# Spreading the normalisation steps of a first projection stage, and reordering the loads of output weights where a recurrent chain begins

## The chip, the cores and the metric

The kernel runs on one core of a Trainium2 chip. The metric is the device time of one launch in microseconds (us). Of several launches the median is compared.

## The reference

Four layers alternate, A B A B, each added to a residual stream of 2048 rows of 640 values. The change touches layer A: a recurrent transformer with memory. Rows come in 64 segments of 32; every segment is preceded by 8 memory rows, which are the first 8 output rows of the segment before.

```python
for s in range(n_seg):                       # 64 segments, one after the other
    xs = x[:, s * seg_len:(s + 1) * seg_len, :]      # x is the layer norm of the stream
    h = jnp.concatenate([mem, xs], axis=1)           # 8 + 32 rows
    q, k, v = (einsum('btd,dhe->bhte', h, W) for W in (Wq, Wk, Wv))   # 32 heads of 192
    scores = jnp.where(mask, einsum('bhqe,bhke->bhqk', q, k) * scale, -1e9)
    o = einsum('bhqk,bhke->bhqe', softmax(scores), v)
    o = einsum('bhte,hed->btd', o, Wo)
    mem = o[:, :M, :]
    outs.append(o[:, M:, :])
```

Layer B is linear attention with softmax features (32 heads of 20) and stays as it is.

## The kernel before

Each layer A has two parts. `A_pre` is a batched stage: it projects the last 8 rows of every segment (the tail rows 24 to 31) to Q, K and V, for all 64 segments at once, so that the chain has only 32 rows left to project per segment: the 8 memory rows and rows 0 to 23. `A_chain` is the chain over the 64 segments.

**The batched stage.** The 64 segments are two halves, h = 0 and 1, of 32 segments; each half's 256 tail rows are gathered from DRAM, normalised (in layer 0 only, where `x_raw` is given), transposed on TensorE (`transpose_rows`, tile `pt`) and stand as `xT[h]` in SBUF. The heads are four rounds r of 8 heads. So there are 8 steps (h, ri): in layer 0 both halves of r = 3, then of r = 2, 1 and 0. This document numbers them 0 to 7. A step projects K, then Q (12 PSUM banks of 10 matmuls of 256 columns, L803), stores both with one DMA from ACT's queue (`kqb`, L809, 1536 KB, from staging buffer `sts[step % 2]`), then V (8 banks of 5 matmuls of 384 columns, L820), stored by POOL's DMAs (`vb`, L824, from the staging buffers `vts`). All matmul banks come from one pool of 8. `evict` copies a bank to its staging buffer, on DVE and ACT in turn (L87 and L89), and then runs one entry of a list `tasks`, if there is one.

In layer 0 that list holds side steps: first the normalisation of the second half's tail rows (`tails`), then that of all 2048 rows in 16 blocks of 128 (`all_rows`), whose result goes to DRAM for the chain. One block is four entries: a starts the load of x on POOL's queue (L755), b takes the moments (DVE L221 and L223, then two casts on POOL, L225 and L227), c takes Ln and Exp on ACT (L234, L235), d applies them on DVE (L241 to L244) and stores (POOL, L756). The entry a of the next block stands ahead of b of this one. Both halves are transposed when their first step begins.

**Weights.** SP's queue loads the matrices in the order of their use, in pieces of 384 KB (L625 for places used once, L619 for the nine slots that r = 3, r = 0 and later the chain share). It runs far ahead of TensorE. `wo_rows` is a copy of two quarters of the output weights Wo (r = 0 and 3) to a DRAM tensor of another layout; it is two DMAs of 1920 KB from ACT's queue (L649), at step 4. The chain then loads Wo in pieces of 320 KB: r = 0 and 3 from `wo_rows` into `wo_end` (L636), r = 1 and 2 from the input into `wo_mid` (L638). During the stage `wo_end` holds `vts` and `xT` and `wo_mid` holds `sts`, so a piece (r, k) can be loaded only when its place comes free. The set `early` names those that are loaded in the last step (`early_wo`); the others are loaded when the chain begins (`late_wo`), ahead of the slots that its first segment needs next. At the chain's first segment, between Q and K of its first round, `fill(FILL[li])` issues short weight loads on TensorE.

**The order of things.** This part of the kernel is scheduled by hand: each engine and queue runs in the order of the program. A DMA from SP or from ACT carries one of eight completion semaphores (`DMAHW0` to `DMAHW7`, shared by both), and the program makes its issue wait until the transfer that had that semaphore before has landed. What stands behind a waiting issue on the same engine waits with it, and on ACT those are copies out of PSUM.

Of the kernel before, what the change touches and what calls it, by code (L numbers as in the profile page):

```python
# [8 lines left out]
P = 128  # L9
BF16 = mybir.dt.bfloat16  # L10
F32 = mybir.dt.float32
# [8 lines left out]

FILL = {0: 122, 2: 78}
SEG_FILL = 1
# [93 lines left out]
class Kernel:  # L116
# [98 lines left out]

    def ln_moments(self, lp, xt):
        nc, Dm = self.nc, self.Dm
        half = Dm // 2
        stats = lp.tile([P, 2, 6], F32, name="ln_stats")
        for j in range(2):  # L220
            nc.vector.bn_stats(out=stats[:, j, :], in_=xt[:, j * half:(j + 1) * half])  # L221
        mv = lp.tile([P, 2], F32, name="ln_mv")
        nc.vector.bn_aggr(out=mv[:], in_=stats[:])  # L223
        mv16 = lp.tile([P, 2], BF16, name="ln_mv16")
        nc.gpsimd.tensor_copy(out=mv16[:], in_=mv[:])  # L225
        mvr = lp.tile([P, 2], F32, name="ln_mvr")
        nc.gpsimd.tensor_copy(out=mvr[:], in_=mv16[:])  # L227
        return mvr
# [352 lines left out]
    def layer_A(self, xn_dram, at_dram, li, x_raw=None):  # L581
# [46 lines left out]

        early = {(0, 5), (2, 4), (2, 5), (1, 0), (1, 1), (1, 2), (1, 3)}

# [14 lines left out]
        def lay_out_wo():  # L645
            if li == 0:
                self.wo_rows = dram.tile([2, P, 7680], BF16, name="wo_rows")
                for i, r in enumerate((0, 3)):
                    nc.scalar.dma_start(out=self.wo_rows[i].rearrange("p (c m) -> p c m", m=640),  # L649
                                        in_=wov[:, 12 * r:12 * r + 12, :])  # L650

        def early_wo():
            for r in (0, 2, 1):
                load_wo(r, part=[k for k in range(6) if (r, k) in early])

        def late_wo(r):
            load_wo(r, part=[k for k in range(6) if (r, k) not in early])

# [9 lines left out]
    def A_pre(self, xn_dram, li, load_matrix, piece, wo_mid, wo_end, lay_out_wo, early_wo, x_raw):  # L668
# [12 lines left out]
        with ExitStack() as es:  # L681
# [4 lines left out]
            else:  # L686
                es.enter_context(tc.manual_schedule(engines={nc.sync.engine}))
            xT = [wo_end[:, 3584 + 1280 * i:3584 + 1280 * i + 1280] for i in range(2)]
            xB = None
# [22 lines left out]
            def norm_tasks(load, done, tag="ln_xn"):  # L712

                v = {}

                def a():
                    v["x"] = lp.tile([P, self.Dm], BF16, name="ln_x")
                    load(v["x"])

                def b():  # L720
                    v["m"] = self.ln_moments(lp, v["x"])

                def c():
# [18 lines left out]
            def evict(out, in_):  # L742
                ev.copy(out=out, in_=in_)
                if tasks:
                    tasks.pop(0)()

            normed = {}

            def tails(h):
                return in_turn([norm_tasks(lambda x, k=k: gather(x, x_raw, h, k),  # L750
                                           lambda xn, k=k: normed.__setitem__((h, k), xn), "ln_xt") for k in range(NT)])

            def all_rows():
                rows = [slice(P * b, P * b + P) for b in range(self.NB)]
                return in_turn([norm_tasks(lambda x, q=q: nc.gpsimd.dma_start(out=x[:], in_=x_raw[q, :]),  # L755
                                           lambda xn, q=q: nc.gpsimd.dma_start(out=xn_dram[q, :], in_=xn[:]))  # L756
                                for q in rows])
# [15 lines left out]
            for h, ri, r in steps:  # L773
                if h not in seen:
                    seen.add(h)
                    xBT = columns(h)
                    for k in range(NT):
                        if x_raw is not None:
                            xb = normed[h, k]
                        else:  # L780
                            xb = xB[h][k % 2]
                            gather(xb, xn_dram, h, k)
                        transpose_rows(xb, h, k)
                xBT = columns(h)
                if (h, ri) == ((NH - 1, 0) if x_raw is None else (0, 2)):
                    lay_out_wo()
# [27 lines left out]
                for k in range(NT):  # L814
                    vt = vts[nv % 2]
                    nv += 1
                    for g in range(4):
                        ps = ps_.tile([P, 512], F32, name="ps_pre", tag="bank")
                        for b in range(KC):
                            nc.tensor.matmul(ps[:, 0:384], lhsT=xBT[:, b, P * k:P * k + P],  # L820
                                             rhs=w[b][:, 384 * g:384 * g + 384], start=(b == 0), stop=(b == KC - 1))
# [8 lines left out]
    def A_chain(self, xn_dram, at_dram, li, load_slot, piece, load_wo, late_wo, wo_mid, wo_end, low):  # L830
# [3 lines left out]
        with tc.tile_pool(name=f"A{li}_ch", reuse_waits="tile", bufs=1) as sp, \  # L834
# [358 lines left out]
```

## Time and profile before

| | us |
|---|---|
| median of 4 runs (3764.53 to 3778.69) | 3772.76 |
| the profiled execution: its time | 3764.53 |
| the profiled execution: its span | 3762.8 |
| layer 0: batched stage, from the first projection to the chain's first matmul | 11.26 to 197.46 |
| layer 0: the chain's first segment | 197.46 to 234.07 |
| its second segment | 234.07 to 255.01 |
| layer 2: end of the batched stage, and the chain's first segment | 2061.18, 2061.18 to 2097.56 |

Times within the profile are us from the span's start. Step 5, 6 and 7 of the batched stage start at 138.56, 158.16 and 177.76. The span's time and the launch's time differ by 1.7 us.

### The profile page before, as it was taken

How to read it: one execution, taken by the hardware profiler on the slowest of the kernel's cores; microseconds unless marked ns; L12 is line 12 of the kernel's file. 1: busy time of each engine (PE TensorE's matmuls, PEld its weight loads, DVE VectorE, ACT ScalarE, POOL GpSimd, SP SyncE). 2: the span in 40 equal slices, each digit the busy share in tenths (PEclk: the TensorE clock that was granted, in tenths of full speed). 3: DMA queues.
4: the chain of work that ended last, by engine and by line, in shares of the span. 5: the costliest groups of instructions: out<-in, count | busy, mean ns of one | idle time of the engine just before them, and what ended most of it. 6: DMA issues, size and time to landing. Idle time of an engine off the chain costs nothing.

```text
span 3762.8 us, 169123 instructions
## 1 busy us (share of the span) xinstructions
PE 3550.7 (94%) x71064; PEld 2322.1 (62%) x71408; DVE 2364.3 (63%) x6290; ACT 2075.1 (55%) x5285; POOL 1660.1 (44%) x4363
## 2 busy tenths in 40 slices
PE   7989999999999999989899899999999999999898
PEld 5756666666666666555377566666666666665453
DVE  5456666666666667546633566666666666664565
ACT  2246566666666656546433556666666666655453
POOL 3345555555555545430333445555545555543400
PEclk9999999999999999989899999999999999999899
DMA  9788788887888878830477888888887888879200
GB/s 348 222 275 290 273 285 289 278 297 271 291 285 286 292 261 296 296 105 1 143 252 203 291 274 293 278 295 276 290 283 271 293 278 288 290 264 309 64 1 29
DMA packets 531381, 931.72 MB, mean 248 GB/s; under 512 B 141034, under 2 KB 298362, under 8 KB 530618
## 3 DMA queue, kind: packets, MB, share of 16 engines
q1 hardware_dynamic: 392794, 802.36, 60.8%
q0 software_dynamic: 68160, 88.78, 8.1%
q10 hardware_dynamic: 69664, 29.76, 3.0%
q8 instruction: 558, 9.14, 1.0%
q14 instruction: 205, 1.68, 0.1%
HBM read 852.43 MB, written 72.09 MB: 246 GB/s over the span
## 4 chain that ended last, share of the span: by engine, by line
PE 55%; DMA 16%; DVE 7%; issue 7%; ACT 6%; PEld 5%; POOL 3%; SPq 1%; POOLq 0%; ACTq 0%; DVEq 0%
PE ps_qk L901 18%; DMA arena<-wo_rows 8%; PE ps_w L977 7%; PE ps_v L901 7%; PE ps_o L951 4%; PE ps_s L943 4%; PEld L803 3%; DMA arena<-in_A_Wv_dram 3%; PE ps_s L1009 2%; PE ps_idle L984 2%; PE ps_s L938 2%; DVE hT L857 2%; PE ps_qk L388 2%; DMA Vp<-vb 1%; PE ps_pre L803 1%
## 5 line engine op out<-in xcount | busy, mean ns | idle before, releaser
L901 PE MATMUL ps_qk<-arena,hT 128*32 128x384 bf16 x20480 | 1001.8, 328 | 25.0 <-DMA arena<-in_A_Wk_dram 11.4
L901 PEld LDWEIGHTS <-hT 128*32 128x32 bf16 x30720 | 738.9, 96 | 443.4 <-DVE hT L1119 27.0
L911 ACT ACTIVATE raw<-ps_qk 128x384 bf16<-128x384 f32 x1024 | 503.1, 491 | 399.0 <-PE ps_s L1009 248.8
L977 PE MATMUL ps_w<-arena,OT 128*32 128x160 bf16 x24576 | 546.9, 235 | 27.9 <-issue 15.8
L884 POOL DMA_DIRECT2D Vp<-vb x512 | 258.8, 506 | 671.7 <-PE ps_o L951 460.1
L901 PE MATMUL ps_v<-arena,hT 128*32 128x384 bf16 x10240 | 535.1, 329 | 0.0
L977 PEld LDWEIGHTS <-OT 128*32 128x32 bf16 x24576 | 437.2, 97 | 123.9 <-issue 46.3
L916 DVE STREAM_TRANSPOSE KT<-raw 128x384 bf16<-128x384 bf16 x512 | 296.1, 578 | 205.3 <-ACT raw L911 201.3
L919 DVE STREAM_TRANSPOSE QT<-raw 128x256 bf16<-128x256 bf16 x512 | 227.9, 445 | 240.2 <-ACT raw L911 199.5
L872 POOL DMA_DIRECT2D kqb<-kqb x512 | 286.1, 559 | 162.9 <-POOL KT L880 148.5
L932 DVE CAST Vp<-ps_v 64x384 bf16<-64x384 f32 x512 | 286.1, 559 | 88.9 <-ACT Vp L930 75.6
L970 POOL DMA_DIRECT2D otb<-otb x512 | 282.9, 552 | 121.5 <-DVE otb L966 101.9
L930 ACT ACTIVATE Vp<-ps_v 64x384 bf16<-64x384 f32 x512 | 246.3, 481 | 144.2 <-PE ps_v L901 108.2
L957 DVE CAST OT<-ps_o 128x192 bf16<-128x192 f32 x512 | 183.2, 358 | 221.9 <-PE ps_o L951 204.8
L1016 DVE TENSOR_TENSOR E<-E,ps_s 80x320 bf16<-80x320 bf16 x512 | 247.4, 483 | 73.5 <-ACT ps_s L1015 69.4
L995 ACT ACTIVATE E<-ps_s 80x320 bf16<-80x320 f32 x512 | 221.8, 433 | 127.0 <-PE ps_s L943 99.4
L951 PEld LDWEIGHTS <-Vp 80*128 80x128 bf16 x4096 | 184.1, 99 | 156.6 <-issue 121.5
L951 PE MATMUL ps_o<-E,Vp 80*128 80x80 bf16 x4096 | 234.2, 202 | 25.1 <-DMA Vp<-vb 5.1
L943 PE MATMUL ps_s<-QT,KT 128*80 128x80 bf16 (+1 forms) x3072 | 233.7, 213 | 24.1 <-DVE KT L916 13.6
L956 ACT ACTIVATE OT<-ps_o 128x192 bf16<-128x192 f32 x512 | 167.9, 328 | 142.8 <-PE ps_o L951 142.7
L865 ACT ACTIVATE Vp<-ps_w 32x160 bf16<-32x160 f32 x512 | 150.7, 294 | 172.3 <-DVE wt L1118 154.4
L943 PEld LDWEIGHTS <-KT 128*80 128x80 bf16 x3072 | 195.6, 119 | 72.8 <-issue 60.9
(148 smaller groups left out, 5465.0 us busy)
## 6 DMA issues: line engine op xcount, KB each, us to landing
arena<-wo_rows SPq DMA_DIRECT2D x792, 320.0 KB, 6.9
arena<-in_A_Wq_dram SPq DMA_DIRECT2D x427, 384.0 KB, 4.6
arena<-in_A_Wv_dram SPq DMA_DIRECT2D x427, 384.0 KB, 6.4
arena<-in_A_Wk_dram SPq DMA_DIRECT2D x768, 192.0 KB, 4.8
kqb<-arena ACTq DMA_DIRECT2D x16, 1536.0 KB, 12.3
kqb<-kqb POOLq DMA_DIRECT2D x512, 48.0 KB, 5.1
arena<-in_A_Wk_dram SPq DMA_DIRECT2D x43, 384.0 KB, 6.8
vb<-arena POOLq DMA_DIRECT2D x128, 112.0 KB, 5.4
```

Of the source, the lines that this page charges most:

```text
L872: nc.gpsimd.dma_start(out=kqb[:], in_=self.kqb_d[s, :, r, :])
L884: nc.gpsimd.dma_start(out=Vs[n % 2][64:80, :], in_=self.vb_d[s, r].rearrange("g t f -> (g t) f"))
L901: nc.tensor.matmul(o[32 * g:32 * g + 32, 0:384], lhsT=hT[:, b, :], rhs=rhs, start=(i == 0), stop=(i == KC - 1), tile_position=(0, 32 * g), ...
L911: nc.scalar.activation(out=raw[:], in_=ps[:, 0:384], func=ACT.Copy)
L916: nc.vector.transpose(out=KT[:, :, 0:64], in_=raw[:, :].rearrange("p (c j) -> p c j", j=64))
L930: nc.scalar.activation(out=o, in_=i, func=ACT.Copy)
L932: nc.vector.tensor_copy(out=o, in_=i)
L943: nc.tensor.matmul(S[0:80, c0:c0 + 80 * (q1 - q0)], lhsT=KT[:, 3 * x + i, :], rhs=QT[:, x, q0:q1, :], start=False, stop=(x == 1 and i == 2 ...
L951: nc.tensor.matmul(O[x][:, 80 * i:80 * i + 80], lhsT=Vs[n % 2][0:80, 448 * x + k:448 * x + k + 128], rhs=E[0:80, 160 * x + 80 * e:160 * x ...
L970: nc.gpsimd.dma_start(out=self.otb_d[s, :, 96 * r:96 * r + 96], in_=otb[:, :, :].rearrange("p c t -> p (c t)"))
L977: nc.tensor.matmul(W[32 * g:32 * g + 32, 0:160], lhsT=OT[:, c, q:q + 32], rhs=w[:, 640 * i + 160 * g:640 * i + 160 * g + 160], start=(firs ...
L1016: nc.vector.tensor_tensor(out=E[0:80, 0:320], in0=E[0:80, 0:320], in1=rc, op=ALU.mult)
```

## The change

Five things change. (1) The side steps are thinned: `all_rows` gets an empty entry after every second one and begins in step 1, not in step 0, and `tails` gets three empty entries between its loads and its moments. (2) The two small casts of the moments move from POOL to DVE. (3) TensorE gets dummy matmuls: 12 before the first transposes, 3 after each of the first two; and the second half's rows are transposed in the middle of step 0's V (after its first four banks). (4) `wo_rows` is written from SP's queue and one step later in the program, ahead of the loads for r = 0. (5) The two `xT` are placed anew in `wo_end`, so that piece (0, 4) of Wo is free in the last step and joins `early`; the early pieces are loaded in the order 2, 0, 1; at the chain's beginning piece (0, 3) goes first, then the rest of r = 1, then pieces 0 to 2 of r = 0. `FILL[0]` goes from 122 to 86. Layer 2 shares (5) apart from the fill.

```diff
-FILL = {0: 122, 2: 78}
+FILL = {0: 86, 2: 78}
...
-        nc.gpsimd.tensor_copy(out=mv16[:], in_=mv[:])
+        cast = cast or nc.gpsimd
+        cast.tensor_copy(out=mv16[:], in_=mv[:])
...
-        nc.gpsimd.tensor_copy(out=mvr[:], in_=mv16[:])
+        cast.tensor_copy(out=mvr[:], in_=mv16[:])
...
-        early = {(0, 5), (2, 4), (2, 5), (1, 0), (1, 1), (1, 2), (1, 3)}
+        early = {(0, 4), (0, 5), (2, 4), (2, 5), (1, 0), (1, 1), (1, 2), (1, 3)}
...
-                    nc.scalar.dma_start(out=self.wo_rows[i].rearrange("p (c m) -> p c m", m=640),
+                    (nc.sync if x_raw is not None else nc.scalar).dma_start(out=self.wo_rows[i].rearrange("p (c m) -> p c m", m=640),
                                         in_=wov[:, 12 * r:12 * r + 12, :])
...
-            for r in (0, 2, 1):
+            for r in (2, 0, 1):
                 load_wo(r, part=[k for k in range(6) if (r, k) in early])
...
-            xT = [wo_end[:, 3584 + 1280 * i:3584 + 1280 * i + 1280] for i in range(2)]
+            xT = [wo_end[:, 5120 - 1280 * i:6400 - 1280 * i] for i in range(2)]
...
-                    v["m"] = self.ln_moments(lp, v["x"])
+                    v["m"] = self.ln_moments(lp, v["x"], nc.vector)
...
-                if tasks:
-                    tasks.pop(0)()
+                step = tasks.pop(0) if tasks else None
+                if step:
+                    step()
...
+                return t[:NT] + [None] * 3 + t[NT:]
...
+                return [f for i in range(0, len(t), 2) for f in (*t[i:i + 2], None)]
...
+                warm = ps_.tile([P, 512], F32, name="ps_warm", tag="bank")
+
+                def busy(n):
+                    for _ in range(n):
+                        nc.tensor.matmul(warm[:, :], lhsT=self.ident[:, :], rhs=vts[0].rearrange("p g f -> p (g f)")[:, 0:512],
+                                         start=True, stop=True, skip_group_check=True)
+
+                busy(12)
...
-                if h not in seen:
+                if h not in seen and (x_raw is None or h == 0):
...
                         transpose_rows(xb, h, k)
+                        if x_raw is not None:
+                            busy(3)
...
-                if (h, ri) == ((NH - 1, 0) if x_raw is None else (0, 2)):
+                if (h, ri) == ((NH - 1, 0) if x_raw is None else (NH - 1, 2)):
                     lay_out_wo()
...
+                if x_raw is not None and (h, ri) == (NH - 1, 0):
                     tasks += all_rows()
...
+                    if x_raw is not None and (h, ri, k) == (0, 0, 0):
+                        for h1 in range(1, NH):
+                            for k1 in range(NT):
+                                transpose_rows(normed[h1, k1], h1, k1)
...
-            for r in (0, 1):
-                late_wo(r)
+            late_wo(0, [3])
+            late_wo(1)
+            late_wo(0, range(3))
```

More of the change, by code (lines that the diff above doesn't have):

```diff
@@ L214, in ln_rows, with ln_moments @@
         self.ln_apply(lp, xt, m, self.ln_deviation(lp, m), xn, centre, scale)
-    def ln_moments(self, lp, xt):
+    def ln_moments(self, lp, xt, cast=None):
         nc, Dm = self.nc, self.Dm
@@ L648, in lay_out_wo, with late_wo @@
                 for i, r in enumerate((0, 3)):
-                    nc.scalar.dma_start(out=self.wo_rows[i].rearrange("p (c m) -> p c m", m=640),
+                    (nc.sync if x_raw is not None else nc.scalar).dma_start(out=self.wo_rows[i].rearrange("p (c m) -> p c m", m=640),
                                         in_=wov[:, 12 * r:12 * r + 12, :])
         def early_wo():
-            for r in (0, 2, 1):
+            for r in (2, 0, 1):
                 load_wo(r, part=[k for k in range(6) if (r, k) in early])
-        def late_wo(r):
-            load_wo(r, part=[k for k in range(6) if (r, k) not in early])
+        def late_wo(r, part=range(6)):
+            load_wo(r, part=[k for k in part if (r, k) not in early])
         self.A_pre(xn_dram, li, load_matrix, piece, wo_mid, wo_end, lay_out_wo, early_wo, x_raw)
@@ L743, in evict @@
                 ev.copy(out=out, in_=in_)
-                if tasks:
-                    tasks.pop(0)()
+                step = tasks.pop(0) if tasks else None
+                if step:
+                    step()
             normed = {}
             def tails(h):
-                return in_turn([norm_tasks(lambda x, k=k: gather(x, x_raw, h, k),
-                                           lambda xn, k=k: normed.__setitem__((h, k), xn), "ln_xt") for k in range(NT)])
+                t = in_turn([norm_tasks(lambda x, k=k: gather(x, x_raw, h, k),
+                                        lambda xn, k=k: normed.__setitem__((h, k), xn), "ln_xt") for k in range(NT)])
+                return t[:NT] + [None] * 3 + t[NT:]
             def all_rows():
                 rows = [slice(P * b, P * b + P) for b in range(self.NB)]
-                return in_turn([norm_tasks(lambda x, q=q: nc.gpsimd.dma_start(out=x[:], in_=x_raw[q, :]),
-                                           lambda xn, q=q: nc.gpsimd.dma_start(out=xn_dram[q, :], in_=xn[:]))
-                                for q in rows])
+                t = in_turn([norm_tasks(lambda x, q=q: nc.gpsimd.dma_start(out=x[:], in_=x_raw[q, :]),
+                                        lambda xn, q=q: nc.gpsimd.dma_start(out=xn_dram[q, :], in_=xn[:]))
+                             for q in rows])
+                return [f for i in range(0, len(t), 2) for f in (*t[i:i + 2], None)]
             for vt in vts:
```

## The prediction

> **What bounds the kernel now.** The page comes first. Busy shares alone say TensorE:
>
> ```profile
> PE 3550.7 (94%) x71064; PEld 2322.1 (62%) x71408; DVE 2364.3 (63%) x6290; ACT 2075.1 (55%) x5285; POOL 1660.1 (44%) x4363
> ```
>
> The change touches two places, so I went to their stretches. The timeline of TensorE over layer 0's batched stage:
>
> ```profile
> 11.26 15.98 PE L803 MATMUL ps_pre<-arena 128*128 128x256 bf16 x120 [0.79 <-ACT arena L89]
> 27.08 6.66 PE L820 MATMUL ps_pre<-arena 128*128 128x384 bf16 x40
> 33.58 0.72 PE L166 MATMUL pt<-ident,ln_xt 128*128 128x128 bf16 x10
> 41.99 15.98 PE L803 MATMUL ps_pre<-arena 128*128 128x256 bf16 x120 [7.69 <-ACT arena L89]
> ...
> 64.30 3.44 PE L803 MATMUL ps_pre<-arena 128*128 128x256 bf16 x30
> 68.59 9.98 PE L803 MATMUL ps_pre<-arena 128*128 128x256 bf16 x90 [0.85 <-ACT arena L89]
> ...
> 177.76 13.26 PE L803 MATMUL ps_pre<-arena 128*128 128x256 bf16 x120
> 190.86 6.66 PE L820 MATMUL ps_pre<-arena 128*128 128x384 bf16 x40
> 197.46 1.00 PE L901 MATMUL ps_qk<-arena,hT 128*32 128x384 bf16 x20
> ```
>
> Columns: start, length, what. An undisturbed step takes 197.46 - 177.76 = 19.6 to 19.7 us. Steps 0 and 1 take 22.3 each, with 7.7 us of nothing between them; steps 2 to 4 (64.30 to 138.56) take 74.3 where three would take 58.8. The ideal end is 10.8 + 8 x 19.6 + 0.7 = 168.3: 29 us are there to be won.
>
> What could stand in the way? The table by stretches (PE, granted clock, DMA share, GB/s), and ACT's timeline at one stall:
>
> ```profile
> 40.00:60.00 20.00, 18.01 (x134) 0.81 0.97 349
> 60.00:80.00 20.00, 17.82 (x149) 1.00 1.04 402
> 100.00:120.00 20.00, 17.94 (x136) 1.00 0.62 177
> 160.00:180.00 20.00, 20.00 (x166) 1.00 0.50 130
> ```
>
> ```profile
> 60.43 0.21 ACT L235 ACTIVATE ln_sd<-ln_lv 128x1 bf16<-128x1 f32 x1
> 67.13 0.39 ACTq L809 DMA_DIRECT2D kqb<-arena  x1
> 68.05 0.87 ACT L89 ACTIVATE arena<-ps_pre 128x384 bf16<-128x384 f32 x2 [7.41 <-DMA ln_x<-in_A_x_dram]
> ```
>
> The DMA engines are full from 10 to about 86 us, because SP loads far ahead. And ACT stood still from 60.64 to 67.13: it wanted to issue step 1's store, whose completion semaphore was held by a Wv load of r = 1 that landed at 67.06. So the store of a step is tied to SP's stream of loads. At the chain's beginning SP is late:
>
> ```profile
> 201.67 4.52 SPq L636 DMA_DIRECT2D arena<-wo_rows  x5
> 206.28 0.90 SPq L638 DMA_DIRECT2D arena<-in_A_Wo_dram  x2
> 207.23 2.36 SPq L619 DMA_DIRECT2D arena<-in_A_Wq_dram  x3
> ```
>
> ```profile
> 214.40 0.35 PE L901 MATMUL ps_qk<-arena,hT 128*32 128x384 bf16 x4 [1.41 <-DMA arena<-in_A_Wq_dram]
> 222.71 0.51 PE L901 MATMUL ps_qk<-arena,hT 128*32 128x384 bf16 x4 [4.57 <-DMA arena<-in_A_Wk_dram]
> ```
>
> **The change, part by part.**
>
> *Warm-up, casts, early transposes.* The second `pt` waits for moments that go DVE, POOL, ACT: POOL's two casts stand from 7.50 to 8.21; two small DVE operations (nearest row: a 128x1 reciprocal, 0.11 to 0.17) take 0.3, so step 0 starts at 10.8 instead of 11.26. Twelve 512-column matmuls cost 4.9 us at the half clock (26 of 256 columns took 5.3 us at clock 0.50), from 2.0, when the memset of `vts` ends, to 6.9, ahead of the 8.2 at which TensorE was first wanted. After idle time K and Q cost 15.98 instead of 13.26: 2.7 us, gone at steps 0 and 1 with the 7.7 us gap. The Trainium skill, page "TensorE: Matmul & The Clock Gate", Part 1, gives a half-rate phase of about 3.4 us, which would cost 1.7; the trace's 2.7 is used. DVE's added casts (16 x 0.3 us) hide: DVE is busy 13.4 of 20 us at its fullest stretch.
>
> *Thinned side steps.* Per block DVE needs 0.88 + 0.21 + 0.16 + 0.37 + 0.39 + 0.3 = 2.3 us, now against six evictions instead of four: 3 x 0.69 + 2.3 = 4.4 of 6.6 us. The load of x gets eight evictions (8 us) of lead instead of five, against its 5.5 to 6 us of landing, which had stopped DVE for 9.8 us between 64 and 138. The 15.5 us of steps 2 to 4 should go.
>
> *What then is late.* TensorE runs ahead, SP's stream doesn't. Two stores now meet it; I read from the program's order which load holds their semaphores.
> Hold 1, step 1's store: wanted at 45, held by the fourth Wq load of r = 1. Before, that load (issued 51.37) landed near 61. The loads ahead of it wait for step 0's store, which is issued at 24.9 instead of 31.53 but shares full engines with two more loads and `vb`; it landed at 44.60, and I take 45 to 46 again. With fewer x blocks in between, the load lands near 59. TensorE can run on for V (6.5) and four K banks (4.4) past 44.2, to 55.1; with the 1.5 us that a held store took to restart TensorE (67.06 to 68.59) it resumes at 60.5, cold. Eight banks, 8 x 1.1 + 2.7, end step 2's K and Q at 72.0.
> Hold 2, step 2's store: wanted at 72.8, held by the last K load of r = 0, now behind `wo_rows` in SP's queue. Before, 58 matrix loads had landed at 86.14. This one is the 50th, so eight fewer: 8 x 0.393 MB x 2.61 us/MB (20.84 MB took 71.6% of 76 us) = 8.2 us less. `wo_rows` is 3.93 MB at 2.96 us/MB (2.57 MB took 84.4% of 9 us, 124 to 133) = 11.6 more. Two x blocks fewer: 1.6 less. So it lands at 88. TensorE runs on for V and three banks to 81.8, resumes at 89.5, cold. Step 3 ends 9.9 + 2.7 + 6.5 later at 108.6, four steps more make 187.0. Against 197.46: 10 us of the 29.
> Here a rule speaks against the edit. The trace's share of 1.04 beside 0.50 later says that `wo_rows` moves from empty engines to full ones. The Trainium skill, "DMA: Bandwidth & Descriptors", section "Issuing engines are not separate DMA queues", says that DMAs from any engine run on the same 16 DMA engines and interleave, and that another issuer saves only issue time. Were SP's queue to hide the copy, the load would land at 76.4, inside the run-on, and the stage would end at 72.0 + 6.5 + 5 x 19.6 = 176.5. By the rule and the shares it is 187; I take that.
> What ACT saves, 4.29 + 2.99 us of issuing at 115 to 122.5, removes TensorE waits of 1.70 and 1.05, already counted in the 15.5; SP's queue issues it at 60 to 68 instead, and only loads for r = 0 stand behind, with hold 2 among them.
>
> *Chain's beginning.* With T = 197.46, the first Wq load was issued at T + 9.8, after five pieces that waited for `vb` (T + 4.2 and T + 6.9) and two more. Now (0, 3) goes at T, r = 1 at T + 2.0 (step 7's store landed at 199.48), and Wq after (0, 1) and (0, 2) at T + 7.8: 2 us sooner, and idle DMA time before T + 4 is used. The wait for Wk, 4.57, shrinks accordingly; I take 2.5 (2 to 3.3). In layer 2 the first Wq went at T + 10.96: 3. The fill's 36 fewer loads (1.90 / 122 x 36 = 0.56 us) end in the same wait for Wk: nothing; if that cover were gone, 0.6. The new order of early pieces: they were issued at 134 to 182 and used after 209: nothing.
>
> *Sum.* 10 + 2.5 + 3 = 15.5. Against the profiled execution: 3764.5 - 15.5 = 3749. That execution is the fastest of four, 8 below the median, so the median to expect is 3772.8 - 15.5 = 3757.
>
> **The rivals.**
> *No holds.* The stores find their semaphores free, or TensorE's run-on covers them. Then all 29 us come, and 5.5: 3738. For it: the run-on is 10 to 11 us, and hold 1 is only 5 us beyond it. Against: a full DMA system. 0.2.
> *Side steps still bite, or the loads land later.* If half of the 15.5 us stays after hold 2 or the load lands at 96, the gain is 15.5 - 8: 3765. For it: POOL's queue still mixes `vb` stores and x loads. 0.19.
> *Slower.* The held store at step 2 pays one us for each us that the K load is later than 88. At 103.5 nothing is left, at 115 the kernel is 0.3% slower (3784). That needs 38 us for `wo_rows`. Against: from its issue at 115.19 it took 18.6 us with a store and `vb` beside it. For: stores have landed 23.3 us after issue in the full stretch (67.13 to 90.44). 0.05.
> That the edits don't do what they say is hardly open: the program's order shows the new places.
>
> **How the numbers follow.** A measurement of this kernel tells about 0.3% (11.3 us) from no change. The main case has 0.56, 3750 to 3765 by its bounds; three quarters of it lie beyond 11.3 us of gain. Faster: 0.42 + 0.2 + 0.02 = 0.64. Slower 0.05. The same: 0.31. The range reaches from no holds, 3738, to the weak case with the spread of medians, 3770.
>
> **What would show it.** Right: TensorE's timeline with K and Q of step 0 at 13.3, no gap before step 1, two gaps of 5 to 8 us near 55 and 82, each with an `ACTq` row of `kqb` right after; steps of 19.6 after about 108; the chain's first matmul near 187; Wq at the chain 2 us sooner. Wrong: steps of 19.6 throughout (no holds), a chain that starts after 192, or waits of DVE for x loads in steps 3 to 5.

## The result, and the profile after

The changed kernel takes 3760.08 us (median of 36 runs, 3747.92 to 3772.91), the kernel before 3769.6 us (57 runs). The ratio is 0.9975, with a 95% interval of 0.9968 to 0.9981: 9.4 us faster, 7 to 12 by the interval. Forecast were 15.5 us of gain. The profiled execution took 3759.21 us, with a span of 3757.1.

TensorE's timeline of layer 0's batched stage (start, length, what; in brackets the idle time before and what ended it):

```profile
10.75 13.40 PE L818 MATMUL ps_pre<-arena 128*128 128x256 bf16 x120
...
31.05 13.26 PE L818 MATMUL ps_pre<-arena 128*128 128x256 bf16 x120
...
50.65 4.53 PE L818 MATMUL ps_pre<-arena 128*128 128x256 bf16 x40
62.95 11.26 PE L818 MATMUL ps_pre<-arena 128*128 128x256 bf16 x80 [7.77 <-ACT arena L89]
...
82.78 2.34 PE L818 MATMUL ps_pre<-arena 128*128 128x256 bf16 x20 [0.97 <-DVE arena L87]
92.90 12.73 PE L818 MATMUL ps_pre<-arena 128*128 128x256 bf16 x90 [7.78 <-ACT arena L89]
113.47 13.26 PE L818 MATMUL ps_pre<-arena 128*128 128x256 bf16 x120
...
191.97 1.00 PE L920 MATMUL ps_qk<-arena,hT 128*32 128x384 bf16 x20
```

K and Q of step 0 are down from 15.98 to 13.40, and the gap ahead of step 1 is gone. Two gaps of 7.8 us stand where the forecast put them, after four K banks of step 2 and after three of step 3 (10 matmuls each), and both restarts are cold (granted clock 0.52 from 62.95 to 68, 0.50 from 92.9 to 98): 90 matmuls take 12.73 instead of 9.98. From 113.47 on a step takes 19.6 (the next ones start at 133.07, 152.67 and 172.27). The chain starts at 191.97, 5.5 us sooner than before; forecast was 187.0.

ACT's timeline names the gaps (`ACTq` is its queue issuing a DMA):

```profile
61.82 0.38 ACTq L824 DMA_DIRECT2D kqb<-arena  x1
62.41 0.87 ACT L89 ACTIVATE arena<-ps_pre 128x384 bf16<-128x384 f32 x2 [15.36 <-DMA arena<-in_A_Wq_dram]
...
91.80 0.37 ACTq L824 DMA_DIRECT2D kqb<-arena  x1
92.36 0.49 ACT L89 ACTIVATE arena<-ps_pre 128x384 bf16<-128x384 f32 x1 [17.34 <-DMA arena<-in_A_Wk_dram]
```

ACT stood 15.4 and 17.3 us ahead of the two stores, and what ended each wait was a load of SP: of Wq at 61.8 (hold 1) and of Wk at 91.7 (hold 2). The two copies of `wo_rows`, issued at 60.76 and 62.72, landed at 77.79 and 86.14, and four K loads for r = 0 behind them at 88.34, 89.47, 90.59 and 91.70.

The beginning of the chain, from TensorE's timeline:

```profile
204.20 0.32 PE L996 MATMUL ps_w<-arena,OT 128*32 128x160 bf16 x8 [1.25 <-DMA arena<-wo_rows]
...
207.71 0.35 PE L920 MATMUL ps_qk<-arena,hT 128*32 128x384 bf16 x4 [0.61 <-DMA arena<-in_A_Wq_dram]
...
214.00 0.51 PE L920 MATMUL ps_qk<-arena,hT 128*32 128x384 bf16 x4 [3.55 <-DMA arena<-in_A_Wk_dram]
```

The waits for Wq and Wk are shorter than before (0.61 and 3.55 instead of 1.41 and 4.57), and the longest wait for `wo_rows` is longer (1.25 instead of 0.64). The first segment took 34.04 us instead of 36.61 in layer 0 and 35.07 instead of 36.38 in layer 2. In sum: 5.5 + 2.6 + 1.3 = 9.4 us, the median's gain, and closer to it than single traces warrant (below). The two profiled executions as wholes differ by 5.3 us only (3764.53 and 3759.21). Stretches that the change hardly touches differ between them by as much, both ways: the stretch between the two chains is 4.5 us longer in the changed one, the other segments of layer 2's chain are 7 us shorter.

### The profile page after: what moved, and what is told of

It is laid out like the page before. It is cut to its first block, busy times and chain, and to the rows that moved or that the text cites. A ratio compares the mean times of both kernels' runs of the same rounds, so it can differ in the third digit from the quotient of the medians.

```text
span 3757.1 us, 169092 instructions
## 1 busy us (share of the span) xinstructions
PE 3560.4 (95%) x71082; PEld 2322.7 (62%) x71390; DVE 2369.5 (63%) x6330; ACT 2074.4 (55%) x5285; POOL 1658.0 (44%) x4323
## 3 DMA queue, kind: packets, MB, share of 16 engines
q8 instruction: 558, 9.14, 1.0%
```

## The experiments

The theory was that two stores held on ACT by SP's loads eat most of the 29 us that the stage could give, and that `wo_rows` ahead of the loads for r = 0 lengthens the second. The rivals: the DMA engines are simply full; side steps or POOL's queue bound the stage; the gain comes from elsewhere. This table holds what each run gave. "Chain starts" is the first matmul of layer 0's chain in the profiled execution; the next columns are the lengths of the first segment of layer 0 and of layer 2. Gains are (1 - ratio) x the median of before on the same chip (3772 for e1 to e8, 3752.7 for e9 to e12: chips differ, so only ratios are compared). Parts (1) and (2) of the change and the early transposes were not undone one by one; that the side steps' waits went is read from the timelines alone.

| | ratio to before, 95% interval | gain, us | chain starts | first segments |
|---|---|---|---|---|
| before | | | 197.46 | 36.61, 36.38 |
| changed kernel | 0.9975, 0.9968 to 0.9981 | 9.4 | 191.97 | 34.04, 35.07 |
| e1 wo_rows on ACT again | 0.9935, 0.9921 to 0.9949 | 24.5 | 186.54 | 35.20, 34.20 |
| e2 wo_rows behind r = 0 | 0.9952, 0.9940 to 0.9964 | 18.1 | 184.16 | 36.72, 34.56 |
| e3 store later on ACT | 0.9959, 0.9946 to 0.9972 | 15.5 | 188.60 | 41.40, 35.17 |
| e4 all stores on POOL | 0.9947, 0.9932 to 0.9962 | 20.0 | 196.58 | 25.40, 36.63 |
| e5 before with part (5), fill 86 | 1.0332, 1.0312 to 1.0351 | -125 | 198.65 | 34.07, 34.61 |
| e6 e2, stores 1 to 3 on POOL | 0.9944, 0.9928 to 0.9960 | 21.1 | 181.49 | 37.20, 34.11 |
| e7 no dummy matmuls | 1.0284, 1.0264 to 1.0304 | -107 | 186.51 | 34.04, 33.30 |
| e8 Wk ahead of Wo r = 2 | 0.9963, 0.9948 to 0.9977 | 14.0 | 191.16 | 34.48, 35.41 |
| e9 e5 with fill 122 | 0.9994, 0.9982 to 1.0005 | 2.3 | 199.84 | 35.72, 37.92 |
| e10 e7 with fill 122 | 0.9971, 0.9959 to 0.9983 | 10.9 | 185.51 | 34.57, 33.52 |
| e11 changed kernel, fill 122 | 1.0209, 1.0186 to 1.0231 | -78 | 194.41 | 37.45, 35.16 |
| e12 e6 thinned twice | 0.9907, 0.9889 to 0.9924 | 34.9 | 169.20 | 36.08, 34.29 |

How far single executions scatter can be read from kernels whose stage is the same: the changed kernel, e8 and e11 start the chain at 191.97, 191.16 and 194.41; e5 and e9 at 198.65 and 199.84; e7 and e10 at 186.51 and 185.51. So a difference of 2 to 3 us between two traces is not a finding here.

**e1: `wo_rows` back on ACT.**

```diff
-                    (nc.sync if x_raw is not None else nc.scalar).dma_start(out=self.wo_rows[i]...
+                    nc.scalar.dma_start(out=self.wo_rows[i]...
...
-                if (h, ri) == (... else (NH - 1, 2)):
+                if (h, ri) == (... else (0, 2)):
                     lay_out_wo()
```

> The changed kernel with one part undone: the two DMAs of wo_rows go from ACT's queue again, at step 4, where they were before. In the program's order step 1's store is now tied to a Wv load of r = 1 (three loads later than the Wq load of the changed kernel), step 2's to the first-to-last Wq load of r = 0, six loads behind the last K load of r = 0. Theory (stores held by the completion semaphores of SP's loads): hold 1 is 3 us longer (gap near 58 about 11 us); without 3.93 MB ahead of them the r = 0 loads land some 11 us sooner and hold 2 ends near 86, inside TensorE's run-on, so the gap of 7.8 us near 85 goes with its 2.7 us of cold clock; ACT's 7.3 us of issuing at step 4 give 2 to 3 us back. Stage ends at 185 to 188 instead of 192.0, gain over the kernel before 13 to 16 us instead of 9.5. Rival (the weights themselves come too late on full DMA engines, whatever the store waits for): the gap near 85 shrinks likewise, but hold 1's gap does not grow; stage ends near 182. Rival (wo_rows on ACT costs its whole issue time in TensorE time): stage ends at 192 or later, gain 9 or less.

The chain started at 186.54, within the 185 to 188 that the theory gave, and at step 3 waits of 1.14 and 4.07, both for DVE, stood in the place of the 7.78. The sign at hold 1 went against the theory: its gap was 7.80, not about 11, as the bandwidth rival had it (but that rival's end, 182, missed). The Wv load that held the store landed at 63.17, only 1.4 us after the changed kernel's Wq load, and TensorE itself came 1.4 us later. So part (4) of the change, taken alone, cost 5 us at the stage's end. The median's gain of 24.5 is 10 us more than stage and first segments of this trace explain (10.9 + 1.4 + 2.2); the profiled execution was the slowest of its six (3757.74). That rest isn't placed.

**e2: `wo_rows` on SP, but behind the loads for r = 0.**

```diff
                 load_matrix("V", r)
+                if x_raw is not None and (h, ri) == (0, NR - 1):
+                    lay_out_wo()
```

> The changed kernel with wo_rows still on SP's queue, but issued behind the loads for r = 0 (after step 6's load of V) instead of ahead of them. Holds as in the run before: step 1's store is tied to a Wv load of r = 1, step 2's to a Wq load of r = 0. Theory (held stores): hold 1 about 3 us longer, hold 2 inside TensorE's run-on, no issue time on ACT; stage ends at 183 to 185, gain over the kernel before 16 to 18 us. Rival (DMA engines' load decides, 3.93 MB more anywhere in the full stretch cost the same): the copy still runs at 65 to 95 us beside step 2's store and vb, stage ends within 1 us of 192 and the gain stays at 9 to 10.

TensorE's timeline of e2:

```profile
64.35 10.94 PE L818 MATMUL ps_pre<-arena 128*128 128x256 bf16 x80 [9.15 <-ACT arena L89]
75.12 6.66 PE L837 MATMUL ps_pre<-arena 128*128 128x384 bf16 x40
81.62 1.25 PE L818 MATMUL ps_pre<-arena 128*128 128x256 bf16 x10
84.06 12.17 PE L818 MATMUL ps_pre<-arena 128*128 128x256 bf16 x110 [1.19 <-DVE arena L87]
96.07 1.79 PE L837 MATMUL ps_pre<-arena 128*128 128x384 bf16 x10
100.79 5.04 PE L837 MATMUL ps_pre<-arena 128*128 128x384 bf16 x30 [2.93 <-DVE arena L87]
```

Hold 1 grew (9.15, half of the 3 us expected), hold 2 left 1.19, and a wait of 2.93 for DVE, which the theory had not named, came at step 3's V. The chain starts at 184.16, as expected. The same 3.93 MB moved behind 15 loads of 384 KB gave 7.8 us, so it is their place in SP's queue that counts, not the bytes as such. Of the 7.8 us, layer 0's first segment gave 2.7 back. It waits for weights as long as in the changed kernel (7.9 and 8.0 us), but its matmuls are busy 27.7 us instead of 24.8, at a mean clock of 0.81 instead of 0.85.

**e3: the store later in ACT's program.** The issue of `kqb` stands behind V's eight banks.

```diff
-                nc.scalar.dma_start(out=self.kqb_d[SH * h:...], in_=st)      # behind Q
+                    if x_raw is not None and k == NT - 1:                    # behind V's last bank
+                        nc.scalar.dma_start(out=self.kqb_d[SH * h:...], in_=st)
```

> The changed kernel with ACT's issue of the kqb store moved in layer 0's stage from behind Q's banks to behind V's eight banks of the same step, 6.5 us later in TensorE's time. wo_rows stays on SP ahead of r = 0. Step 1's store is tied to the same fourth Wq load of r = 1 as in the changed kernel, step 2's to the second-to-last K load of r = 0. Theory (held stores): the same loads land at the same time, near 60 and 88 to 91, but ACT arrives at the wait 6.5 us later, so the run-on that TensorE has behind V is still whole; each gap of 7.8 us falls to 0 to 3 us and at least one cold restart (2.7) goes: stage ends at 175 to 181, gain over the kernel before 20 to 26 us. Rival (weights late, the store only coincides): TensorE waits at the same times for its weights, stage ends within 2 us of 192, gain 8 to 11. Rival (sts comes free later, so that step n+2's evictions wait for the late store): new waits of ACT or DVE on kqb of 3 to 10 us, stage ends at 185 or later.

The main expectation missed. Hold 1 did shrink to 2.06 us, but at step 3 TensorE stood for 14.21. The waits view of e3, 50 to 110 us (us in total, times, longest):

```profile
DVE arena L87 <- DMA kqb<-arena: 18.8, 2, 17.1
...
ACT arena L89 <- DMA arena<-in_A_Wq_dram: 9.8, 1, 9.8
```

Step 1's store went out at 64.31 and gave its staging buffer back to step 3's copies only at 95.98 (the end of DVE's 17.1). The wait itself ended at 64.31 and not near 60, because step 0's store, now issued at 31.90, landed at 57.06, and until then SP stood with a load of r = 1 that needed its semaphore. So the tie works both ways: a store holds SP's loads, and these loads hold the next store. The third theory (`sts` comes free later) is what decided. The stage and the two first segments of this trace (41.40 in layer 0, with a wait of 8.4 us for `wo_rows`) explain 5 of the 15.5 us of gain; the rest isn't placed.

**e4: the stores from POOL.**

```diff
-                nc.scalar.dma_start(out=self.kqb_d[SH * h:...
+                (nc.gpsimd if x_raw is not None else nc.scalar).dma_start(out=self.kqb_d[SH * h:...
```

> The changed kernel with the kqb store of layer 0's stage issued from POOL's queue instead of ACT's, at the same place. Its completion semaphore is then one that only POOL's own DMAs (vb, x) use, so no load of SP can hold it, and a wait stops POOL, not the copies out of PSUM. Theory (held stores): no gap near 58 or 85, steps of 19.6 to 20.5 throughout; stage ends at 170 to 178, gain over the kernel before 23 to 31 us. Rival (weights late on full engines): gaps remain, now as waits of TensorE on Wk, Wq or Wv, stage ends at 185 to 192. Rival (POOL becomes the bound: its vb stores and x loads stand behind the wait for the store's semaphore, so vts comes free late and V's copies wait): waits of ACT and DVE on vb of 2 us a step or more, stage ends at 180 to 195.

TensorE's timeline of e4:

```profile
49.10 9.39 PE L835 MATMUL ps_pre<-arena 128*128 128x384 bf16 x40 [5.09 <-DVE arena L87]
58.32 11.08 PE L818 MATMUL ps_pre<-arena 128*128 128x256 bf16 x100
...
175.27 6.66 PE L835 MATMUL ps_pre<-arena 128*128 128x384 bf16 x40
196.58 1.79 PE L920 MATMUL ps_qk<-arena,hT 128*32 128x384 bf16 x20 [14.64 <-DVE hT L876]
```

No gap from ACT is left, and the projections end at 181.9, 10 us sooner than in the changed kernel. But POOL pays: DVE waited up to 12.0 us for an x block whose load stood in POOL's queue behind `vb` and step 0's store, which gave the 5.09; and at the end the chain's first loads, POOL's too, stood behind step 7's store: 14.64. The first segment then took only 25.40, with no wait for weights left in it. The theory was right on the gaps and wrong on the end (170 to 178) and the gain (23 to 31); the rival of POOL's queue was right that this queue becomes the bound, though what came late was x and the chain's loads, and not `vts`.

**e5 and e9: part (5) alone, with two values of the fill.** e5 is the kernel before with part (5); e9 is e5 with one number back:

```diff
-FILL = {0: 86, 2: 78}
+FILL = {0: 122, 2: 78}
```

> The kernel before with part (5) of the change alone: xT placed anew, piece (0, 4) early, the new order of early and late pieces, FILL[0] 86. Theory (the chain's beginning is worth its own 4 us in any kernel): the batched stage ends at 197.5 within 1 us, layer 0's first segment takes 34.0 to 34.5 us instead of 36.61, layer 2's 35.0 to 35.3 instead of 36.38; gain 3.5 to 4 us. Rival (the first segment only became shorter since the stage's end was disturbed otherwise): both segments as before within 0.5 us, gain 0 to 1 us. Rival (the fill of 36 fewer loads is no longer covered by the wait for Wk): layer 0 gains 0.6 us more than layer 2's difference explains.

> e5 with FILL[0] back at 122, and nothing else. In e5 each segment of the chain was about 1 us longer than before, with a stop of TensorE of 1.4 us at the 24th of the 48 output matmuls (L977) in 120 of the 126 segments, for which the trace names no releaser. TensorE's program has 1024 instructions per segment, and 36 fewer ahead of the chain in e5 than in the kernel before. Theory (the place of the chain's instructions in TensorE's instruction stream decides: something that happens at fixed places of the stream falls into the burst of output matmuls): with 122 the count ahead of the chain is that of the kernel before, the stops at matmul 24 vanish, and part (5) alone gives 2 to 4 us of gain. Rival (part (5)'s order of loads slows the chain, by other completion semaphores for example): still over 100 us slower.

e5 was 3.3% slower, which no theory had foreseen, and e9 was not. The loss lies in the chain: segment by segment e5's trace falls behind by about 1 us. One row each from the costliest groups, first e5, then e9 (busy, mean ns, idle time before and its releaser):

```profile
L977 PE MATMUL ps_w<-arena,OT 128*32 128x160 bf16 x24576 | 559.0, 236 | 149.3 <-issue 143.4
```

```profile
L977 PE MATMUL ps_w<-arena,OT 128*32 128x160 bf16 x24576 | 537.3, 234 | 21.4 <-issue 11.4
```

The output matmuls (bursts of 48 in 1 us, four to a segment) are the same in number and length, but 143 us of idle time stand ahead of them in e5 for which the profile names no releaser. Two segments of e5, TensorE's output matmuls:

```profile
611.20 0.58 PE L977 MATMUL ps_w<-arena,OT 128*32 128x160 bf16 x23
612.33 0.66 PE L977 MATMUL ps_w<-arena,OT 128*32 128x160 bf16 x25 [0.54 <-issue]
...
632.69 0.59 PE L977 MATMUL ps_w<-arena,OT 128*32 128x160 bf16 x23
633.52 0.66 PE L977 MATMUL ps_w<-arena,OT 128*32 128x160 bf16 x25 [0.25 <-issue]
```

Always after the 23rd, in the third burst of the segment. What recurs at a fixed place of the program and has no releaser? The page has a queue that none of the kernel's DMAs use (packets, MB, share of the engines); the line is that of e5, e9 and both kernels alike:

```profile
q8 instruction: 558, 9.14, 1.0%
```

9.14 MB over the 142,452 matmuls and weight loads of e5 are 64 bytes each, and 9.14 MB in 558 packets are 16.4 KB, or 256 instructions, each. A segment of the chain has 1024 instructions of TensorE in the program, so four packets, and their edges fall at the same four places of every segment. The count ahead of the chain sets which. The Trainium skill, "Runtime: NRT & Kernel Launch", section "Instruction fetch mechanics", says that a queue of its own brings an engine's instructions in blocks of 16 KiB, 256 instructions, and that crossing a block's edge is "mostly hidden". The trace agrees with the size; on the cost the measurement differs: one edge 36 instructions further on was 3.4% of this kernel. In e9 and the changed kernel the stop is at the 6th matmul of the burst, 18 matmuls (36 instructions) from the 24th, and it is over 0.3 us in 31 and 39 of the 128 segments, where e5 has 120. That the stop is a wait for this queue shows in the packets' own times: in all 120 of e5, TensorE goes on between 1.18 and 1.70 us (median 1.40) after a packet of queue 8 has ended, and in the changed kernel's 39 between 1.22 and 1.58. Without such a link the delay would be spread over the 5 us from one packet to the next.

What remains of part (5): 2.3 us by e9, -2 to 7 by its interval. Its first segments were 35.72 and 37.92; over all kernels with part (5), layer 0's lie between 34.0 and 37.5 (e3 and e4 aside) and layer 2's between 33.3 and 37.9. Before has one trace. Most of that scatter is the matmuls' own time: TensorE is busy for 24.6 to 28.0 us of layer 0's first segment, at mean clocks of 0.77 to 0.90. What part (5) acts on scatters less: TensorE waits for weights 7.3 to 9.3 us in these segments of layer 0 and 7.1 to 9.6 in layer 2's, against 10.0 and 9.3 before. So in layer 0 the waits are shorter in every trace, by 0.7 to 2.7 us; a gain in the kernel's time of 2 to 4 us is neither shown nor excluded.

**e7 and e10: no dummy matmuls, with two values of the fill.**

```diff
-                busy(12)
...
-                            busy(3)
```

> The changed kernel without its 18 dummy matmuls (12 and 2 x 3). By the program's order this also moves the ties: step 1's store is now held by the third Wq load of r = 1 (one load sooner than in the changed kernel), step 2's by the second K load of r = 0 (three loads sooner than the last one). Theory (what comes ahead of a held store is swallowed by the hold): step 0's K and Q take about 16 us again and step 1 ends 2.7 us later, but TensorE restarts after hold 1 within 1.5 us of the changed kernel's 62.95, and after hold 2 about 3 us sooner, near 89.5; stage ends at 187 to 190, gain over the kernel before 11 to 14 us. Rival (the warm-up's 2.7 us stand on the path to the end): stage ends at 194 to 195, gain 6 to 7 us.

> e7 (no dummy matmuls) with FILL[0] at 122, and nothing else; 18 dummy matmuls are 36 instructions of TensorE (a load and a matmul each), as many as the fill lost. Theory (count of TensorE's instructions): the 105 us are gone; the stage ends near 186.5 as in e7, gain over the kernel before 13 to 16 us, not less than the changed kernel's 9.5, so the dummy matmuls' clock is worth nothing at the stage's end. Rival (the missing warm-up itself slows the kernel): still about 105 us slower.

e7 was 107 us slower, e10 was not: the 18 dummy matmuls are 36 instructions, and `FILL[0]` had been lowered by 36 to keep the chain where it was. With the count restored, the kernel without them gains 10.9 us, 6 to 15, as much as the changed kernel. K and Q of step 0 took 14.71 instead of 13.40, and still the chain started at 185.51. The edit had redrawn the ties: step 1's store hangs on an earlier Wq load, step 2's on the second K load of r = 0; the gaps ahead of the restarts at 60.56 and 87.05 were 2.76 and 4.38. So the warm-up's 1.3 to 2.6 us came ahead of a held store, and the kernel is no slower without it. What it is worth with the ties left as they were is not shown: the earlier ties may move the stage's end by themselves, and of the 13 to 16 us expected of e10 10.9 came.

**e11: the changed kernel with 36 instructions more.**

```diff
-FILL = {0: 86, 2: 78}
+FILL = {0: 122, 2: 78}
```

> The changed kernel with FILL[0] at 122 instead of 86: 36 instructions of TensorE more ahead of the chain. Prediction's term: 0.6 us at most, hidden. Theory (count): the places of the stream fall 36 instructions, that is 18 output matmuls, earlier in each segment: the place that lay at matmul 41 falls at 23, one stop per segment of about 1 us there, 60 to 130 us slower than the kernel before. Rival (only fewer instructions hurt): gain of 9 us as in the changed kernel.

2.1% slower, so more instructions hurt as well as fewer. But the stop was not at matmul 23 of a burst, as I had it. The costliest groups of e11:

```profile
L996 PE MATMUL ps_w<-arena,OT 128*32 128x160 bf16 x24576 | 529.9, 235 | 8.9 <-DMA arena<-wo_rows 8.3
...
L970 PEld LDWEIGHTS <-Vp 80*128 80x128 bf16 x4096 | 186.7, 99 | 236.6 <-issue 192.7
```

The second row in the changed kernel:

```profile
L970 PEld LDWEIGHTS <-Vp 80*128 80x128 bf16 x4096 | 183.5, 99 | 161.4 <-issue 125.2
```

The output bursts are free of these stops, and the loads for `ps_o` have 192.7 us of idle time without a releaser, 67.5 more than in the changed kernel, of the 78 lost against the kernel before: 36 instructions ahead of the 6th output matmul lie in the `ps_o` matmuls before that burst. What I had taken at matmul 41 for a second edge is a wait for the next piece of `wo_rows` (five pieces of eight matmuls are 40).

**e8: Wk ahead of Wo r = 2 at the chain's beginning.**

```diff
                 if s == 0:
-                    late_wo(2)
                     fill(FILL[li])
                 to_rows(q_or_k("K", 0), "K")
+                if s == 0:
+                    late_wo(2)
```

> The changed kernel with one line moved in the chain's first segment of both layers A: the four late pieces of Wo, r = 2, are issued on SP behind the six Wk loads that the first segment waits for, instead of ahead of them (1.31 MB, which at the 375 to 385 GB/s of that stretch are 3.4 to 3.5 us). Theory (the DMA engines are full there, so the order decides and the last Wk ends the wait): the waits for Wk of 3.55 and 3.50 us fall by 2 to 3.5 us each; first segments of 31 to 32 us (layer 0) and 32 to 33 us (layer 2); gain over the kernel before 14 to 16 us. Rival (Wo r = 2 or Wv are late next): new waits for in_A_Wo or in_A_Wv of 2 to 3 us, first segments at most 1 us shorter, gain 10 to 11 us. Rival (the slots of Wk come free too late for an earlier issue): Wk lands as before, gain 9.5 us.

Waits of TensorE in e8, 185 to 230 us:

```profile
PE ps_w L996 <- DMA arena<-wo_rows: 3.0, 4, 1.3
PE ps_v L920 <- DMA arena<-in_A_Wv_dram: 2.8, 2, 2.4
...
PE ps_qk L920 <- DMA arena<-in_A_Wk_dram: 1.0, 1, 1.0
```

The waits for Wk fell from 4.8 to 1.0, and Wv took their place. The first segments are 34.48 and 35.41: no shorter, where 31 to 33 were expected. This suggests that the sum of what the beginning needs decides, and not the order; the rival (Wv is late next) had it so. The gain of 14.0 (9 to 20) cannot be told from the changed kernel's 9.4.

**e6 and e12: the way to the ideal.** e6 is e2 with the stores of steps 1 to 3 alone from POOL; e12 is e6 with an empty entry after every entry of `all_rows`.

```diff
-                nc.scalar.dma_start(out=self.kqb_d[SH * h:...
+                (nc.gpsimd if x_raw is not None and turn in (2, 3, 4) else nc.scalar).dma_start(out=self.kqb_d[SH * h:...
...
-                return [f for i in range(0, len(t), 2) for f in (*t[i:i + 2], None)]      # e12 alone
+                return [f for g in t for f in (g, None)]
```

> The changed kernel with wo_rows behind the loads for r = 0 (as in e2) and the kqb stores of steps 1, 2 and 3 alone issued from POOL; steps 0 and 4 to 7 keep ACT's queue. So no store that is issued while SP's loads fill the DMA engines can hold ACT, except step 0's, whose semaphore was free in time; step 7's store no longer stands in POOL's queue ahead of the chain's first loads. Theory (held stores): no gap near 58 or 85; steps 1 to 3 take 19.6 to 21 us each; stage ends at 172 to 178, end of the first segment 20 to 25 us sooner than in the kernel before, gain 22 to 27 us. Rival (x loads and vb behind the store in POOL's queue, as the 5.1 us in front of step 1's V with all stores on POOL): waits of DVE for x of 3 to 8 us in sum, stage ends at 178 to 184, gain 17 to 22 us. Rival (TensorE then meets weights that have not landed): waits of TensorE for Wk, Wq or Wv of r = 1 or r = 0 at steps 3 to 5.

> e6 with all_rows thinned further: an empty entry after every entry instead of after every second one, so that an x block comes every eight evictions. It takes away half of what e6 suggests is left: DVE waited 32 us for x between 50 and 125, which stopped TensorE for 2.17, 3.07 and 2.10 us with a cold clock after each. Theory (x loads behind the stores in POOL's queue are the next bound): waits of TensorE in steps 2 to 4 fall from 7.8 to under 3 us, stage ends at 174 to 178 instead of 181.5, gain over the kernel before 3 to 7 us more than e6's, if the chain keeps its instruction places. Rival (the chain's beginning then waits for its weights anyway): stage ends as said, but the end of the first segment comes less than 2 us sooner than in e6.

In e6 the holds are gone, and the rival for POOL's queue was right on what is next (17 to 22 us of gain; 21.1 came). Its waits view, 50 to 125 us:

```profile
DVE ln_stats L221 <- DMA ln_x<-in_A_x_dram: 32.0, 8, 8.5
...
POOL ln_x L758 <- DMA kqb<-arena: 6.9, 1, 6.9
```

DVE waited 32 us for x, and TensorE 2.17, 3.07, 0.41 and 2.10 for DVE; the chain starts at 181.49. With the thinner list nothing is left. TensorE's timeline of e12:

```profile
50.14 13.26 PE L818 MATMUL ps_pre<-arena 128*128 128x256 bf16 x120
63.24 6.66 PE L837 MATMUL ps_pre<-arena 128*128 128x384 bf16 x40
69.74 13.26 PE L818 MATMUL ps_pre<-arena 128*128 128x256 bf16 x120
82.84 6.66 PE L837 MATMUL ps_pre<-arena 128*128 128x384 bf16 x40
...
161.24 6.66 PE L837 MATMUL ps_pre<-arena 128*128 128x384 bf16 x40
169.20 1.00 PE L922 MATMUL ps_qk<-arena,hT 128*32 128x384 bf16 x20 [1.30 <-DVE hT L878]
```

Every step takes 19.6, and the chain starts at 169.20; the prediction's ideal was 168.3. That is 5 us better than the 174 to 178 expected, and the end of the first segment came 13.4 us sooner than in e6, so the rival of the chain's beginning falls. e12's table by stretches, and below it the changed kernel's (PE, PEld, DVE, ACT and POOL busy, PE's clock, DMA share, GB/s):

```profile
60.00:80.00 20.00, 20.00 (x166) 16.00 (x164) 11.77 (x28) 5.61 (x13) 10.55 (x31) 1.00 1.03 402
80.00:100.00 20.00, 20.00 (x166) 16.02 (x164) 12.52 (x33) 7.19 (x17) 8.64 (x14) 1.00 1.03 401
```

```profile
60.00:80.00 20.00, 17.05 (x117) 12.54 (x117) 9.33 (x27) 6.12 (x16) 10.05 (x31) 0.80 1.06 383
80.00:100.00 20.00, 11.24 (x75) 8.42 (x73) 7.56 (x22) 4.08 (x11) 4.37 (x8) 0.74 0.94 317
```

The DMA engines are as full as in the changed kernel (1.03), and TensorE doesn't stop. Full engines decide when a load lands; that TensorE stood was the work of the ties, and then of the queue of x. That refutes the rival of engines that are simply full. The gain is 34.9 us, 28 to 42: e12 is the fastest kernel here, 0.993 of the changed one by the two ratios. What thinning alone, without the stores on POOL, would give was not run.

## Why the prediction was right, and where it was off

The mechanism and the places were right: two held stores after the 15.5 us of side steps were won, with TensorE's run-on, cold restarts and undisturbed steps after them. The sum was off by these terms:

- *Hold 1.* Forecast 59 for the landing and 60.5 for the restart; measured 61.8 and 62.95, 2.5 later (61.61 and 63.09 in e8 and e11, where the stage is the same). Step 0's store landed near 48.4 (SP's next load went out at 48.49), not at 45 to 46, and the loads of r = 1 waited for it.
- *Hold 2.* Forecast 88 and 89.5; measured 91.7 and 92.90 (91.57 and 93.69 in e8 and e11). The term that was sized wrong is `wo_rows`: 11.6 us were put down for it. In e1 and e2, where it is not ahead of the load that makes hold 2, that load landed at 73.08 and 72.89, so the copy kept it back by 18.7 us; the forecast without the copy, 76.4, was 3.4 us too late and hid half of this. The issue of the first K load behind the copy alone took SP 8.56 us (69.72 to 78.28); why was not tested. The net, 3.7 us at the load and 3.4 at the restart, reaches the stage's end: what came ahead of hold 2, hold 1's 2.5 included, counts only through SP's stream. That `wo_rows` costs here, as the prediction took it from the shares, e1 and e2 confirm: 5.4 and 7.8 us.
- *Small waits.* 1.23 in step 3's V, for DVE, was not in the sum. With hold 2's 3.4 it makes 4.6 of the 5.0 us between 187.0 and 191.97. The 0.97 ahead of hold 2 was swallowed by it.
- *Warm-up.* 2.6 us at step 0 as forecast, but ahead of hold 1; e10 shows no loss without it. In the sum both restarts are set by loads, so the warm-up buys nothing at the stage's end; the prediction listed it as a gain without saying so.
- *Chain's beginning, layer 0.* 2.6 against 2.5, but not by the path that was forecast: Wq's first load went out at T + 9.6, hardly sooner than the T + 9.8 of before, and not at T + 7.8, since (0, 0) to (0, 2) waited for step 7's `vb` stores. With segments that scatter by 3 us the agreement is luck.
- *Layer 2.* 1.3 instead of 3. Wq's first load went out at T + 10.3 (before T + 10.96), again hardly sooner. The last K matmuls ended their wait 24.9 us after T instead of 27.3, 2.4 sooner; then the same matmuls up to the segment's end took 10.19 us instead of 9.09, at a granted clock of 0.69 instead of 0.80, which gave 1.1 back.
- *The fill.* "Nothing; if that cover were gone, 0.6." Nothing is what the change as a whole pays, but not for the reason given, so the prediction was lucky here. The wait for Wk doesn't hide the fill: its 36 loads balance the 36 instructions of the dummy matmuls, and with only one of the two edits the kernel is 2.1 to 3.3% slower. This is the step whose reasoning failed outright, and a rival with this price (over 100 us) was missing from the list. The program's count of 1024 instructions per segment and the page's row for queue 8 could have raised the suspicion; the price itself only the runs could show.

"Slower" had its chance from a longer hold 2: the load landed at 91.7, where 103.5 would have left nothing.

## What to carry to other kernels

Where engines share completion semaphores, a store is tied to loads that have nothing to do with it: find the load that holds it, and count each edit ahead of a hold as nothing until the hold is gone; full DMA engines alone cost TensorE nothing here (e12). In a program of many equal rounds count TensorE's instructions ahead of them, and keep that count, modulo the 256 instructions of a packet, when you add or take away any, or the edit's own effect drowns. When a hold is removed, look at once at the queue that took the store over: here the x loads behind it were worth another 12 us.

## What the hardware showed unexpectedly

- Where the edge of an instruction packet falls decides what it costs: at the 24th of 48 output matmuls about 1 us per segment (3.3% of the kernel, e5), among the `ps_o` matmuls ahead of that burst 0.6 (2.1%, e11). At the 6th output matmul, between the two, TensorE's idle time there is 0.13 us per segment (17 us over 128 segments in the changed kernel). Why the packet is late at some places and not at others (it shares the DMA engines with 270 GB/s of loads) was not tested.
- A `kqb` store of 1536 KB took 12.5 us from POOL in the full stretch (53.81 to 66.33, in e4), and from ACT 23.2 (91.80 to 115.03) or, in e3, 25.2 (31.90 to 57.06); but from ACT also 13.1 (31.53 to 44.60) and 12.3 (91.24 to 103.56) in the kernel before, so the queue is not shown to be the cause.
- After a hold of 6 to 9 us, a cold restart cost from 1.3 us (80 matmuls in 10.18 instead of 8.84, e11) to 2.8 (90 in 12.73 instead of 9.98, changed kernel). The 2.7 of the forecast lies at the upper end.
- TensorE ran at full clock and without a stop at a DMA share of 1.03 (e12, 60 to 100 us).
- The same kernel before took 3752.7 us on one chip and 3772 on two others.
